# Moving two integer chords of a softmax exponential from VectorE to GpSimd, and sharing TensorE rounds between two groups of heads

## The chip, the cores and the metric

The kernel runs on one core of one Trainium2 chip. The metric is the device time of one execution in microseconds (us), as the median of the runs of a kernel. Each kernel under test was timed next to the kernel before on the same chip. Where runs of different rounds are compared, the kernel before had a median of 788.8 to 789.2 us in each of these rounds. The engines are TensorE (PE in the profile; PEld is its weight load), VectorE (DVE), ScalarE (ACT) and GpSimd (POOL).

## The reference, cut to what matters

One transformer block: layer norm, attention with 32 heads of 16, residual, layer norm, a gated feed-forward layer, residual. 2048 tokens, width 512.

```python
qkv = ...(x @ wqkv)                                # 32 heads of 16
scores = jnp.einsum("bhqd,bhkd->bhqk", q, k) * (Dh ** -0.5)
p = _softmax(scores, axis=-1)                      # 32 x 2048 x 2048 exponentials
o = jnp.einsum("bhqk,bhkd->bhqd", p, v)
...
h = sigmoid(g) * u                                 # F = 1792
```

There are 134 million exponentials. This is what loads ScalarE and VectorE, and the two products around the softmax load TensorE.

## The kernel before

The kernel is a program that plans its own order: while it is built, it keeps a clock per engine (`T["P"]`, `T["D"]`, `T["A"]`, `T["G"]`), adds an assumed duration for each instruction, and from this decides what to issue next. The hardware runs the order that results; it does not see the assumed durations.

A *tile* is (mostly) three *units* of scores in PSUM, each 128 partitions by 512 columns. ScalarE makes the exponentials of two units or of all three in one instruction. Where VectorE has time, it takes the third unit. The kernel computes no exponential there: it writes an affine function of the score as int16 and lets the value product read these bits as fp16, which gives a piecewise linear power of two. Two more copies of it, shifted by +326 and -332 (the *chords*), smooth it: their sum, the last with weight 1.5625, is the exponential. The first exponential and both chords go to TensorE as three inputs, so a unit on VectorE costs TensorE three value products in place of one.

```python
CHORDS, WEIGHT = (326, -332), 1.5625

    GQ, QB = 4, 3                  # four units share a J buffer; three J buffers
    def dexp_first(src, u, n):     # src is PSUM, float32; J is SBUF, int16
        ...
        nc.vector.tensor_scalar(out=J[:, 0, k, :], in0=src, scalar1=ZOFF, scalar2=0.0,
                                op0=ALU.add, op1=ALU.max)
        ...
        if k == GQ - 1:
            dexp_rest()

    def dexp_rest():
        ...
        def chord(s):
            nc.vector.tensor_scalar(out=J[:, s, 0:k, :], in0=J[:, 0, 0:k, :], scalar1=float(CHORDS[s - 1]),
                                    scalar2=0.0, op0=ALU.add, op1=ALU.max)
            for i in range(k):
                quad[i][s].end = T["D"] + TAIL["D"]
        for s in (1, 2):
            chain.append((70 + 133 * k, lambda s=s: chord(s)))
```

A value product has 17 output rows (16 values and the row sum), so four of them, for the four heads of a group, run side by side in four column groups of TensorE (in the timeline their starts lie within 0.02 us of each other). I call such a set a *round*. In the kernel before, a round only takes heads of the current group; at a group's end rounds run with one to three column groups in use.

```python
    def in_rows(uns, limit, full=False):
        ...
            for un in list(left):
                if un.u[3] not in used and len(out) + len(row) < limit:   # u[3]: head 0..3 of the group
                    used.add(un.u[3]); left.remove(un); row.append(un)
            if full and len(row) < live:
                break
```

Four other VectorE instructions are (a) the normalising product of each group, with two SBUF inputs, (b) the two masked copies of each query block, (c) the weighted copy of the value rows, and (d) the application of the second layer norm:

```python
nc.vector.tensor_tensor(out=o2[...], in0=xs[...], in1=rec.to_broadcast(...), op=ALU.mult)              # (a) 60 times
nc.vector.tensor_scalar(out=dst[a][:], in0=qd[:], scalar1=mask[:, a:a + 1], scalar2=None, op0=ALU.mult)  # (b) 30
nc.vector.tensor_scalar(out=Vaug2[:, t], in0=Vaug[:, t], scalar1=WEIGHT, scalar2=None, op0=ALU.mult)     # (c) 16
nc.vector.tensor_scalar(out=hn[:], in0=h[:, i, :], scalar1=mv..., scalar2=rstd..., ...)                  # (d) 14
```

## Time and profile before

| | before |
|---|---|
| median | 788.92 us (788.32 to 789.54, 3 runs) |
| busy share | TensorE 94%, ScalarE 94%, VectorE 90%, GpSimd 4% |
| mean granted TensorE clock | 0.996 |

The page's lines for busy time by engine, and its costliest groups (engine, operation, output and input tile, shapes, count, then busy us and mean ns of one, then idle time just before them):

```profile
PE 740.0 (94%) x11280; PEld 358.3 (45%) x11356; DVE 711.9 (90%) x1406; ACT 737.3 (94%) x780; POOL 31.4 (4%) x67
...
L1321 ACT ACTIVATE pt<-PS 128x1024 f16<-128x1024 f32 (+1 forms) x518 | 541.9, 1138 | 17.8 <-PE PS L1031 11.4
L1177 DVE TENSOR_SCALAR J<-PS 128x512 int16<-128x512 f32 x547 | 363.9, 682 | 34.3 <-PE PS L1154 19.1
...
L1195 DVE TENSOR_SCALAR J<-J 128x2048 int16<-128x2048 int16 (+3 forms) x328 | 185.6, 597 | 1.2
```

The stretch from 200 to 700 us, which is steady attention work (busy us of each engine, number of instructions in brackets; then clock, DMA share, GB/s):

```profile
core 0: us, PE busy (x) PEld busy (x) DVE busy (x) ACT busy (x) POOL busy (x), PEclk, DMA share, GB/s
200.00:700.00 500.00, 479.56 (x8013) 242.64 (x8056) 463.37 (x908) 487.06 (x505) 13.15 (x24) 1.00 0.18 53
```

In 500 us ScalarE works 487, TensorE 480 and VectorE 463. There is no single bound: the plan has filled three engines. The waits view (who waited for whom: us in all, times, longest) shows how little is lost between them:

```profile
ACT pt L1321 <- PE PS L1031: 11.4, 32, 0.7
...
PE PS L1154 <- DVE J L1195: 1.0, 4, 0.3
```

TensorE waited 1.0 us in the whole run for a chord.

### The profile page before, as it was taken

What the parts mean: (1) busy time and instruction counts of PE and PEld (TensorE: products, weight loads), DVE (VectorE), ACT (ScalarE), POOL (GpSimd) and SP (SyncE); (2) the same over time, 40 slices, a digit from 0 to 9 for tenths busy, and PEclk for the clock granted to TensorE, in tenths of its full rate; (3) what the DMA queues carried; (4) which work ended last, traced back from release to release, by engine and by line L of the source; (5) the groups of instructions that cost most, each with busy time, mean ns of one, the idle gap of its engine ahead of it and who ended that gap; (6) DMA issues with size and microseconds to landing.
All of it is one profiled execution on the core that took longest, in us unless ns stands there. A gap on an engine that the chain in (4) does not pass through costs nothing. (4 is left out here: it accounts for less than half of the span.)

```text
span 787.9 us, 25764 instructions
## 1 busy us (share of the span) xinstructions
PE 740.0 (94%) x11280; PEld 358.3 (45%) x11356; DVE 711.9 (90%) x1406; ACT 737.3 (94%) x780; POOL 31.4 (4%) x67
## 2 busy tenths in 40 slices
PE   8889998888999999999999999999999999999997
PEld 3322224444554455444544454435544555444554
DVE  7987999999999899999989899888999898999963
ACT  5989999999999999999999999999999999999962
POOL 4300000001000100000000000100000000100000
PEclk9999999999999999999999999999999999999999
DMA  7000023000131013200312031101211133012160
GB/s 227 1 1 1 1 63 100 3 2 2 56 95 56 9 37 96 61 29 10 95 50 61 16 96 56 37 27 49 83 56 35 36 95 96 8 34 57 56 201 17
DMA packets 66806, 41.56 MB, mean 53 GB/s; under 512 B 3456, under 2 KB 66688, under 8 KB 66688
## 3 DMA queue, kind: packets, MB, share of 16 engines
q1 hardware_dynamic: 66400, 39.59, 16.9%
q8 instruction: 90, 1.47, 0.8%
q10 hardware_dynamic: 288, 0.26, 0.1%
q14 instruction: 28, 0.23, 0.1%
HBM read 37.75 MB, written 2.10 MB: 51 GB/s over the span
## 5 line engine op out<-in xcount | busy, mean ns | idle before, releaser
L1321 ACT ACTIVATE pt<-PS 128x1024 f16<-128x1024 f32 (+1 forms) x518 | 541.9, 1138 | 17.8 <-PE PS L1031 11.4
L1177 DVE TENSOR_SCALAR J<-PS 128x512 int16<-128x512 f32 x547 | 363.9, 682 | 34.3 <-PE PS L1154 19.1
L1154 PE MATMUL PS<-J,Vaug 128*17 128x256 f16 (+1 forms) x2092 | 201.5, 280 | 5.6 <-DVE xs L1097 2.8
L1154 PE MATMUL PS<-pt,Vaug 128*17 128x256 f16 (+1 forms) x2158 | 190.8, 279 | 5.2 <-DVE xs L1097 4.0
L1195 DVE TENSOR_SCALAR J<-J 128x2048 int16<-128x2048 int16 (+3 forms) x328 | 185.6, 597 | 1.2
L1154 PEld LDWEIGHTS <-Vaug 128*17 128x17 bf16 x4886 | 132.9, 90 | 78.3 <-issue 70.8
L1154 PE MATMUL PS<-J,Vaug_100 128*17 128x256 f16 (+1 forms) x1046 | 124.0, 280 | 0.7 <-DVE xs L1097 0.2
L770 PE MATMUL PS<-xnT_82,wgu 128*128 128x256 bf16 x784 | 114.3, 275 | 1.6 <-DVE xnT_82 L761 0.5
L770 PEld LDWEIGHTS <-wgu 128*128 128x128 bf16 x784 | 64.1, 98 | 41.5 <-issue 35.7
L1154 PEld LDWEIGHTS <-Vaug_100 128*17 128x17 bf16 x1046 | 53.6, 90 | 29.6 <-issue 27.3
L1321 ACT ACTIVATE xnT_83<-PS 128x1024 f16<-128x1024 f32 (+1 forms) x52 | 57.4, 1107 | 0.5 <-PE PS L1031 0.4
L788 PE MATMUL PS<-wd,hT 128*128 128x512 bf16 x168 | 50.1, 383 | 2.6 <-issue 2.5
L1031 PEld LDWEIGHTS <-KT_86 32*128 32x128 bf16 x768 | 21.6, 92 | 59.7 <-issue 58.1
L1031 PEld LDWEIGHTS <-KT_87 32*128 32x128 bf16 x1024 | 24.9, 92 | 50.3 <-issue 48.8
L1321 ACT ACTIVATE QTb<-PS 128x1024 f16<-128x1024 f32 x42 | 45.0, 1072 | 0.9 <-PE PS L1031 0.5
L1031 PEld LDWEIGHTS <-KT_88 32*128 32x128 bf16 x1024 | 23.3, 92 | 49.4 <-issue 48.9
L800 ACT ACTIVATE th<-PS 128x512 f32<-128x512 f32 (+1 forms) x63 | 36.4, 577 | 7.5 <-DVE hT L783 6.7
L1031 PE MATMUL PS<-QT_92,KT_87 32*128 32x256 bf16 x512 | 38.2, 272 | 4.5 <-ACT pt L1321 1.9
L1031 PEld LDWEIGHTS <-KT_89 32*128 32x128 bf16 x1024 | 22.8, 92 | 39.4 <-issue 38.9
L1031 PE MATMUL PS<-QT_95,KT_88 32*128 32x256 bf16 x512 | 38.1, 272 | 2.5 <-ACT pt L1321 1.5
L1031 PE MATMUL PS<-QT_93,KT_87 32*128 32x256 bf16 x512 | 37.0, 272 | 2.3 <-ACT pt L1321 1.8
L1031 PE MATMUL PS<-QT_94,KT_88 32*128 32x256 bf16 x512 | 36.1, 272 | 3.0 <-ACT pt L1321 2.5
(288 smaller groups left out, 801.0 us busy)
## 6 DMA issues: line engine op xcount, KB each, us to landing
wgu<-in_B_w_gate_dram SPq DMA_DIRECT2D x49, 256.0 KB, 3.0
wgu<-in_B_w_up_dram SPq DMA_DIRECT2D x49, 256.0 KB, 3.5
out_dram<-ob SPq DMA_DIRECT2D x16, 128.0 KB, 1.7
wd<-in_B_w_down_dram SPq DMA_DIRECT2D x1, 1792.0 KB, 9.2
xr<-in_A_x_dram SPq DMA_DIRECT2D x14, 128.0 KB, 3.5
J<-in_B_w_gate_dram SPq DMA_DIRECT2D x2, 768.0 KB, 4.8
J<-in_B_w_up_dram SPq DMA_DIRECT2D x2, 768.0 KB, 8.2
xb_111<-in_A_x_dram SPq DMA_DIRECT2D x2, 256.0 KB, 4.8
```

The source lines that it names most:

```text
L770: nc.tensor.matmul(ps[:, 0:PARTS[r][2]], lhsT=w[:, d, :], rhs=hn_of(r)[:, d, :], start=(d == 0), stop=(d == DC - 1))
L788: nc.tensor.matmul(ps, lhsT=hT[:, f, i * P:(i + 1) * P], rhs=wd[:, f, :], start=(f == 0), stop=(f == FC - 1))
L800: nc.scalar.activation(out=th[:, 0:ps.shape[-1]], in_=ps, func=ACT.Tanh, scale=0.5)
L1031: nc.tensor.matmul(pss[:, ui, i * CW[qc]:(i + 1) * CW[qc]], lhsT=KT[g // 2][32 * j:32 * j + 32, k * P:(k + 1) * P], rhs=q[32 * j:32 * j + ...
L1154: nc.tensor.matmul(dst[32 * j:32 * j + VW, 0:w], lhsT=un.v[:, kt * SPAN[qc] + i, h, :], rhs=un.ap[:, i * w:(i + 1) * w], start=(c + i == 0 ...
L1177: nc.vector.tensor_scalar(out=J[:, 0, k, :], in0=src, scalar1=ZOFF, scalar2=0.0, op0=ALU.add, op1=ALU.max)
L1195: nc.vector.tensor_scalar(out=J[:, s, 0:k, :], in0=J[:, 0, 0:k, :], scalar1=float(CHORDS[s - 1]), scalar2=0.0, op0=ALU.add, op1=ALU.max)
L1321: ex = nc.scalar.activation(out=pt, in_=pss[:, 0:wa, :], func=ACT.Exp, scale=AS)
```

## The change

The intent: the 328 chord instructions take 185.6 us of VectorE, and GpSimd is 96% idle. If GpSimd makes the chords, VectorE can take more first exponentials (the int16 write from PSUM above) from ScalarE. As the chords then come later, TensorE may fill the rounds of one group's end with heads of the next group, which also saves rounds.

```diff
-    def in_rows(uns, limit, full=False):
+    def in_rows(uns, more, limit, full=False):          # more: units of the next group that are ready
...
+            for un in list(more):
+                j = un.u[3]
+                if (j not in used and len(out) + len(row) < limit
+                        and (due[j] == 0 or not clears and count[gr + (j,)] > 0)):
+                    used.add(j)
+                    more.remove(un)
+                    row.append(un)
...
-                                 rhs=un.ap[:, i * w:(i + 1) * w], start=(c + i == 0),
+                                 rhs=un.ap[:, i * w:(i + 1) * w], start=clears and c + i == 0,
...
+    POOLED, POOL_NS = (1, 2), 470
...
         def chord(s):
+            if s in POOLED:
+                nc.gpsimd.tensor_scalar(out=J[:, s, 0:k, :], in0=J[:, 0, 0:k, :], scalar1=float(CHORDS[s - 1]),
+                                        scalar2=0.0, op0=ALU.add, op1=ALU.max)
+                T["G"] = max(T["G"], quad[-1][0].end + LAT) + POOL_NS * k + 150
+                for i in range(k):
+                    quad[i][s].end = T["G"] + TAIL["G"]
+                return
```

The plan assumes 470 ns for each unit of 512 elements on GpSimd, or 2.03 us for a full chord of four units.

More of the change, by code (lines that the diff above doesn't have):

```diff
@@ L1113, in av_ready, with ahead_ready @@
                 and un.end + LAT <= T["P"] + loose]
-    def in_rows(uns, limit, full=False):
-        out, rows, left = [], 0, list(uns)
-        live = sum(todo[gseq[st["cur"]] + (j,)] > 0 for j in range(4))
-        while left and len(out) < limit:
+    def ahead_ready():
+        i = st["cur"]
+        if i + 1 >= len(gseq) or gseq[i][0] >= NCH:
+            return []
+        j = st["acc"][acc_of(*gseq[i + 1])[1][0]]
+        if j is not None and (j.end is None or j.end + LAT > T["P"] + 60.0):
+            return []
+        return [un for un in avq if un.u[:2] == gseq[i + 1] and un.end is not None
+                and un.end + LAT <= T["P"] + 60.0]
+    def in_rows(uns, more, limit, full=False):
+        out, rows, left = [], 0, list(uns)
+        gr = gseq[st["cur"]]
+        due = {j: todo[gr + (j,)] for j in range(4)}
+        live = 4 if more else sum(n > 0 for n in due.values())
+        more = list(more)
+        clears = more and gseq.index(more[0].u[:2]) % 2 == 0
+        while (left or more) and len(out) < limit:
             row, used = [], set()
@@ L1126, in in_rows @@
                     row.append(un)
-            if full and len(row) < live:
+                    due[un.u[3]] -= 1
+            for un in list(more):
[5 more added lines that the diff above has]
+                    row.append(un)
+            if not row or full and len(row) < live or row[0].u[:2] != gr and len(row) < 4:
                 break
@@ L1133, in av @@
     def av(limit, loose=60.0, full=False):
-        dst, halves = acc_of(*gseq[st["cur"]])
-        busy = [st["acc"][k] for k in halves if st["acc"][k] is not None]
+        busy = [st["acc"][k] for k in acc_of(*gseq[st["cur"]])[1] if st["acc"][k] is not None]
         if any(j.end is None or j.end + LAT > T["P"] + loose for j in busy):
             return 0
-        uns, rows = in_rows(av_ready(loose), limit, full)
+        uns, rows = in_rows(av_ready(loose), ahead_ready(), limit, full)
         if not uns:
@@ L1141, in av @@
         T["P"] = max([T["P"]] + [un.end + LAT for un in uns + busy])
-        for k in halves:
-            st["acc"][k] = None
         for un in uns:
             qc, g, kt, j = un.u
+            dst, halves = acc_of(qc, g)
+            for k in halves:
+                st["acc"][k] = None
             force(("v", kt * SPAN[qc]))
@@ L1152, in av @@
             w = CW[qc]
+            clears = 0 in halves
             for i in range(SPAN[qc]):
                 nc.tensor.matmul(dst[32 * j:32 * j + VW, 0:w], lhsT=un.v[:, kt * SPAN[qc] + i, h, :],
-                                 rhs=un.ap[:, i * w:(i + 1) * w], start=(c + i == 0),
-                                 stop=(todo[qc, g, j] == 0 and i == SPAN[qc] - 1), tile_position=(0, 32 * j))
+                                 rhs=un.ap[:, i * w:(i + 1) * w], start=clears and c + i == 0,
+                                 stop=(todo[qc, g, j] == 0 and i == SPAN[qc] - 1), tile_position=(0, 32 * j),
+                                 skip_group_check=True)
         pe_time("av", MM * rows + 4 * len(uns), 128 * len(uns))
@@ L1160, in av @@
                 un.slot.end = T["P"] + DRAIN
-        qc, g = uns[0].u[:2]
-        if all(todo[qc, g, j] == 0 for j in range(4)):
-            finish_group(qc, g)
+        while st["cur"] < len(gseq) and av_last() == 0:
+            finish_group(*gseq[st["cur"]])
             st["cur"] += 1
@@ L1199, in dexp_rest @@
         for s in (1, 2):
-            chain.append((70 + 133 * k, lambda s=s: chord(s)))
+            if s in POOLED:
+                chord(s)
+            else:
+                chain.append((70 + 133 * k, lambda s=s: chord(s)))
     def pop_chain():
```

## The prediction

> **What bounds it now.** The page gives busy shares of PE 94%, ACT 94%, DVE 90%. By stage (stretch table), from 200 to 700 us ACT is busy 487 of 500 us and PE 479, DVE 463; the granted clock is 0.99 to 1.00. So the attention loop has two saturated engines, TensorE and ScalarE, with VectorE just below; the waits view shows only small waits for VectorE there (PE for the accumulator's transposition 7.5 us in all, PE for the chords J<-J 1.0 us). The last 28 us (tail block) are a serial matmul, tanh and product chain that the change doesn't touch.
>
> **What the change does**, counted in the built instruction orders:
> - VectorE loses 328 chord instructions (185.6 us; 128x2048 takes 0.69 us) and gains 26 first exponentials of 0.68 us (547 to 573; 17.7 us): 712 to about 544 us of work.
> - GpSimd gets the 328 chords (246 of 2048 elements, 32 of 1024, 50 of 512 after regrouping). No chord ran there before. Its one-element TENSOR_SCALAR took 0.34 us. [...]
> - ScalarE: 26 tiles go from 1536 columns (1.50 us) to 1024 (1.06 us): 11.4 us less.
> - TensorE: 94 value matmuls more (each VectorE unit needs three where ScalarE's needs one), but packed better: rounds of up to four column groups fall from 1683 to 1555. A round's starts lie 0.107 us apart in the timeline: 13.7 us less, about 2 us given back to 17 more mode switches.
>
> **How much is on the critical path.** Only the last two: about 11 us on each of the two saturated engines, so about 778 us if idle times stay. The 168 us freed on VectorE are mostly off the path; fewer first exponentials delayed by chord pairs may give some 3 to 5 us of ACT and PE idle back.
>
> Against it: [...] The 60 normalising products (TENSOR_TENSOR, 0.29 us), 32 query splits (0.35 us), 14 layer-norm applies and 16 value copies may each wait about 1 us: perhaps 80 to 100 us on VectorE, most of it absorbed by its new slack, some 5 to 15 us reaching ACT and PE. Chords also arrive 3 to 4 us later than before; the three J buffers are then held longer, and the last group's end may slip 2 us.
>
> Predicted 780 us, 766 to 806. Faster 0.27, same 0.55, slower 0.18.
>
> **What would show it.** GpSimd's J<-J at 2.0 to 2.2 us a full chord, 580 to 630 us busy; VectorE's normalising product and query splits longer than 0.29 and 0.35 us (about 1 us) and bimodal; ACT busy 726 us; PE waits for J from GpSimd under 10 us; first exponentials unchanged at 0.68 us.
>
> **What would make it wrong.** A GpSimd chord of 3 us or more: PE would wait for J and VectorE for free J buffers, 830 us or more. Locked VectorE operations not absorbed: above 800. No blocking and much idle recovered: below 770.

The marked cuts take out of the record the rate on which the forecast of a chord rested, with a second, higher one, and the reason given why VectorE and GpSimd would hold each other up: no trace or run of this case showed them. The sum came to 2.1 us a full chord and some 600 us of GpSimd in all, and the time to 780 us: about 778, with 5 to 15 us of waits and perhaps 2 us at the end against it and 3 to 5 us of idle time for it. The 2 us for 17 mode switches fit the trace: around 400.6 us of the kernel before, the first score product starts 0.21 us after the last round, where rounds start 0.11 us apart. By *blocking* I mean below that a VectorE instruction lasts longer while GpSimd works; a query copy went from 0.35 to 7.16 us in the changed kernel.

## The result, and the profile after

| | before | after |
|---|---|---|
| median | 789.08 us (788.32 to 789.54, 4 runs) | 2160.05 us (2159.68 to 2160.40, 4 runs) |
| ratio | | 2.738 (95% interval 2.733 to 2.742) |
| GpSimd busy | 4% | 95% |
| mean granted TensorE clock | 0.996 | 0.627 |

The changed kernel is 2.74 times as slow, far outside the predicted range of 766 to 806 us.

The page after: busy line, the granted clock in 40 slices, the chain that ended last by engine, and the groups that answer to those shown of before:

```profile
PE 1162.4 (54%) x11373; PEld 427.9 (20%) x11451; DVE 845.3 (39%) x1104; ACT 773.2 (36%) x780; POOL 2057.7 (95%) x411
...
PEclk9865655555565666667566676566556667665557
...
POOL 74%; issue 16%; DVE 5%; PE 4%; ACT 0%; POOLq 0%; DVEq 0%; ACTq 0%
...
L1222 POOL TENSOR_SCALAR J<-J 128x2048 int16<-128x2048 int16 (+3 forms) x344 | 2030.9, 5940 | 43.0 <-DVE J L1203 42.9
L1357 ACT ACTIVATE pt<-PS 128x1024 f16<-128x1024 f32 (+1 forms) x518 | 555.3, 1086 | 1069.1 <-PE PS L1031 1037.4
L1203 DVE TENSOR_SCALAR J<-PS 128x512 int16<-128x512 f32 x573 | 389.1, 686 | 942.8 <-PE PS L1031 587.2
L1179 PE MATMUL PS<-J,Vaug 128*17 128x256 f16 (+1 forms) x2186 | 334.1, 383 | 409.0 <-POOL J L1222 408.2
```

Three things are to be seen. GpSimd is busy 2058 of 2158 us, and 74% of the chain that ended last runs over its chords. Every other engine idles: ScalarE's exponentials now wait for 1069 us in all, the first exponentials on VectorE for 943 us. And the granted TensorE clock, 0.9 or more throughout before, is 0.5 to 0.7 in most slices.

The chords by shape, and who waited:

```profile
L1222 POOL TENSOR_SCALAR J<-J 128x2048 int16<-128x2048 int16 x246 | 1737.6, 7093 | 43.0 <-DVE J L1203 42.9
L1222 POOL TENSOR_SCALAR J<-J 128x1024 int16<-128x1024 int16 x32 | 115.6, 3630 | 0.0
L1222 POOL TENSOR_SCALAR J<-J 128x512 int16<-128x512 int16 x50 | 95.3, 1927 | 0.0
L1222 POOL TENSOR_SCALAR J<-J 128x1536 int16<-128x1536 int16 x16 | 85.8, 5382 | 0.0
```

```profile
ACT pt L1357 <- PE PS L1031: 1037.4, 345, 23.2
PE PS L1179 <- POOL J L1222: 880.0, 276, 10.1
DVE J L1203 <- PE PS L1031: 587.2, 261, 16.9
```

A full chord takes 7.09 us and not 2.0 to 2.2. The four shapes lie on a line: (7093 - 1927) / 1536 = 3.36 ns an element, and about 0.2 us fixed. TensorE waits 880 us for GpSimd where it had waited 1.0 us for VectorE's chords. The kernel issues TensorE's instructions in one order, so the score products (L1031) behind a waiting value product come late too: the other two lines show ScalarE's exponentials and VectorE's first exponentials waiting for them.

The sum closes. 344 chord records at 5.94 us are 2.04 ms, of 2.158 ms. The forecast had the same shapes, but for the 16 of 1536 elements, at 580 to 630 us.

### The profile page after: what moved, and what is told of

The parts are those of the page before. It is cut to its first block, busy times and chain, and to the rows that moved or that the text cites. A ratio compares the mean times of both kernels' runs of the same rounds, so it can differ in the third digit from the quotient of the medians.

```text
span 2157.8 us, 26193 instructions
## 1 busy us (share of the span) xinstructions
PE 1162.4 (54%) x11373; PEld 427.9 (20%) x11451; DVE 845.3 (39%) x1104; ACT 773.2 (36%) x780; POOL 2057.7 (95%) x411
## 4 chain that ended last, share of the span: by engine, by line
POOL 74%; issue 16%; DVE 5%; PE 4%; ACT 0%; POOLq 0%; DVEq 0%; ACTq 0%
POOL J L1222 74%; PE PS L1179 1%; DVE Vaug_100 L297 1%; DVE J L1203 1%; PE PS L770 1%; PE PS L1031 1%; DVE QT_93 L300 1%; DVE Vaug L296 0%; DVE st L260 0%; PE PS L788 0%; PE PS L1504 0%; PE PS L439 0%; DVE QT_95 L300 0%; POOL rstd L268 0%; PE PS L287 0%
## 5 line engine op out<-in xcount | busy, mean ns | idle before, releaser
L1222 POOL TENSOR_SCALAR J<-J 128x2048 int16<-128x2048 int16 (+3 forms) x344 | 2030.9, 5940 | 43.0 <-DVE J L1203 42.9
L1179 PE MATMUL PS<-J,Vaug 128*17 128x256 f16 (+1 forms) x2186 | 334.1, 383 | 409.0 <-POOL J L1222 408.2
L1179 PE MATMUL PS<-J,Vaug_100 128*17 128x256 f16 (+1 forms) x1093 | 192.1, 384 | 472.1 <-POOL J L1222 471.8
L1179 PE MATMUL PS<-pt,Vaug 128*17 128x256 f16 (+1 forms) x2119 | 323.0, 383 | 9.7 <-DVE xs L1097 8.5
L1179 PEld LDWEIGHTS <-Vaug 128*17 128x17 bf16 x4933 | 173.3, 108 | 600.7 <-issue 572.9
L770 PE MATMUL PS<-xnT_82,wgu 128*128 128x256 bf16 x784 | 180.1, 384 | 0.0
L1357 ACT ACTIVATE xnT_83<-PS 128x1024 f16<-128x1024 f32 (+1 forms) x50 | 53.4, 1067 | 77.2 <-PE PS L1031 77.1
L1357 ACT ACTIVATE xnT_84<-PS 128x1024 f16<-128x1024 f32 (+1 forms) x38 | 40.2, 1058 | 70.3 <-PE PS L1031 70.2
L1031 PE MATMUL PS<-QT_92,KT_87 32*128 32x256 bf16 x512 | 55.7, 383 | 17.1 <-DVE J L1203 15.9
L1031 PE MATMUL PS<-QT_94,KT_88 32*128 32x256 bf16 x512 | 52.6, 376 | 12.7 <-DVE J L1203 12.2
L1031 PE MATMUL PS<-QT_97,KT_89 32*128 32x256 bf16 x512 | 51.8, 372 | 11.6 <-DVE J L1203 10.1
L1031 PE MATMUL PS<-QT_96,KT_89 32*128 32x256 bf16 x512 | 51.7, 369 | 9.2 <-DVE J L1203 8.8
L1031 PE MATMUL PS<-QT_95,KT_88 32*128 32x256 bf16 x512 | 52.4, 369 | 6.5 <-DVE J L1203 4.1
L1068 DVE TENSOR_TENSOR o_1_105<-xs,rsum 128x128 bf16<-128x128 f32 x32 | 53.8, 1680 | 1.1
L753 DVE TENSOR_SCALAR hn<-h,mv,rstd 128x512 bf16<-128x512 f32 x14 | 39.2, 2802 | 37.6 <-POOL rstd L268 37.6
```

The source lines that it names most:

```text
L770: nc.tensor.matmul(ps[:, 0:PARTS[r][2]], lhsT=w[:, d, :], rhs=hn_of(r)[:, d, :], start=(d == 0), stop=(d == DC - 1))
L1031: nc.tensor.matmul(pss[:, ui, i * CW[qc]:(i + 1) * CW[qc]], lhsT=KT[g // 2][32 * j:32 * j + 32, k * P:(k + 1) * P], rhs=q[32 * j:32 * j + ...
L1068: nc.vector.tensor_tensor(out=o2[:, 0:w // 32, DH * a:DH * a + DH], in0=xs[:, 0:w // 32, 0:DH], in1=rec.to_broadcast([P, w // 32, DH]), op ...
L1179: nc.tensor.matmul(dst[32 * j:32 * j + VW, 0:w], lhsT=un.v[:, kt * SPAN[qc] + i, h, :], rhs=un.ap[:, i * w:(i + 1) * w], start=clears and ...
L1222: nc.gpsimd.tensor_scalar(out=J[:, s, 0:k, :], in0=J[:, 0, 0:k, :], scalar1=float(CHORDS[s - 1]), scalar2=0.0, op0=ALU.add, op1=ALU.max)
L1357: ex = nc.scalar.activation(out=pt, in_=pss[:, 0:wa, :], func=ACT.Exp, scale=AS)
```

## The experiments

Two theories were on the table at first. Theory A: GpSimd's own time for this instruction is 3.4 times the forecast 2.1 us, and this alone makes the result. Rival B: GpSimd is slow because busy VectorE holds it up. Two more had to be excluded: that the shared rounds do harm, and that the order, planned with a false duration, does the harm. Later the question was what the other terms of the prediction were worth. All kernels gave results that passed the comparison with the reference, but see e5 for how much that says.

### e1: the shared rounds alone

```diff
-    POOLED, POOL_NS = (1, 2), 470
+    POOLED, POOL_NS = (), 470
```

> Changed kernel with both chords back on VectorE: only the sharing of rounds is left. Built order: 1553 rounds of up to four column groups against 1683 (13.9 us of TensorE at 0.107 us a round), 545 first exponentials on VectorE against 547 (ScalarE +0.9 us). If TensorE ends the wait in the loop: about 776 to 780 us. If ScalarE is the nearer bound: 786 to 789 us. If the sharing itself had a hidden cost[...], part of the 2160 us would show here: above 795 us. Theory (GpSimd alone is the cause) says 776 to 789.

Measured: 779.53 us (4 runs) against 788.77; ratio 0.989 (0.987 to 0.990). The page's busy line and the same stretch as above:

```profile
PE 741.4 (95%) x11350; PEld 348.8 (45%) x11350; DVE 708.4 (91%) x1402; ACT 734.9 (95%) x780; POOL 29.7 (4%) x67
```

```profile
200.00:700.00 500.00, 485.31 (x8200) 239.83 (x8197) 471.39 (x921) 493.15 (x514) 12.42 (x24) 1.00 0.19 54
```

The shared rounds are harmless and give 9 us; as an estimate, 130 saved rounds at 0.107 us, the distance of their starts in the timeline, are worth 13.9 us on TensorE. In the stretch, ScalarE went from 487 to 493 us of 500 and TensorE from 480 to 485: the saved rounds let the other engines be used better, until ScalarE has hardly any idle time left. So the whole slowdown comes with the chords on GpSimd.

### e2: one chord on GpSimd

```diff
-    POOLED, POOL_NS = (1, 2), 470
+    POOLED, POOL_NS = (2,), 470
```

> Only the third chord on GpSimd (118 full chords and smaller ones, 578 units of 512). Theory A, GpSimd's own rate of 0.164 us + 3.36 ns an element bounds the kernel: 1.02 ms of GpSimd work, span 1100 us if VectorE's second chords don't get in the way; if each of them ([...]0.69 us alone) waits[...] until a GpSimd chord ends, they show some 4 to 7 us each and the span is 1150 to 1350 us. Rival B, GpSimd is slow because of the traffic of the other engines: the full chord is clearly not 7.05 us here, as VectorE is busier than in the changed kernel.

Measured: 1435.45 us, one run. That is above the expected 1150 to 1350. The groups by shape:

```profile
L1222 POOL TENSOR_SCALAR J<-J 128x2048 int16<-128x2048 int16 x118 | 860.9, 7301 | 256.5 <-DVE J L1203 225.3 <-DVE rsum L1067 31.3
...
L1228 DVE TENSOR_SCALAR J<-J 128x2048 int16<-128x2048 int16 x118 | 317.7, 2694 | 1.7
```

The GpSimd chord is 7.30 us here against 7.09, though VectorE is busy for 79% of the span and not 39% (holds included): nothing for rival B. The new fact is the second line. VectorE's own full chord took 0.69 us before and takes 2.69 us on average here (up to 7.58 us), in a run in which GpSimd is busy for 76% of the span and not 4%: it is held. I had expected 4 to 7 us for each; the median over all shapes is only 0.93 us, so at least half were hardly held. The span is longer than expected: GpSimd sat idle 256 us before its full chords, 225 of them waiting for a first exponential on VectorE. That the two take turns fits this, but no run separates it.

### e3: a plan with the true duration

```diff
-    POOLED, POOL_NS = (1, 2), 470
+    POOLED, POOL_NS = (1, 2), 1720
```

> Both chords on GpSimd, but the kernel's planner is told 1720 ns a unit in place of 470. It then gives VectorE 361 first exponentials in place of 573 and ScalarE the rest (about +80 us against before). Theory A: GpSimd work 722 units x 1.72 us = 1.27 ms, span 1290 to 1360 us, GpSimd above 93% busy, chord still 7.05 us. If the 2160 us came from a bad order (the plan's wrong figure) more than from the rate: span near ScalarE's 820 us.

Measured: 1443.76 us, one run; GpSimd busy 1307.8 us (91%), full chord 7.09 us. With the true figure the plan gives VectorE 361 units in place of 573, and the time falls by a third, because a good third less is asked of GpSimd (722 units in place of 1146). It stays far from ScalarE's 824 us. So the plan's wrong figure is not the cause: the order can only choose how many chords to pay for. The time is above the expected 1290 to 1360 us and GpSimd's share below the expected 93%: the estimate left out 134 us in which GpSimd did nothing, 75 of them waiting for VectorE's first exponentials.

### e4: single GpSimd instructions, behind the end of the kernel

Behind the end of the kernel before, a row of instructions on scratch tiles:

```diff
+    ts(I16, I16, 2048)                          # add, max: the chord
+    ts(I16, I16, 1024)
+    ts(I16, I16, 2048, op1=None)                # add alone
+    ts(I16, I16, 2048, op1=None, op0=ALU.max)   # max alone
+    G.tensor_copy(out=dst[I16][:], in_=src[I16][:])
+    ts(BF16, BF16, 2048); ts(FP16, FP16, 2048); ts(FP32, FP32, 2048); ts(I32, I32, 2048) ...
+    G.tensor_tensor(out=dst[I32][:, 0:1024], in0=src[I32][:, 0:1024], in1=src[I32][:, 1024:2048], op=ALU.add) ...
```

> The kernel before, with a row of single GpSimd instructions behind its end, where every other engine is idle. Theory A: int16 add+max of 2048 elements again 7.0 to 7.1 us, of 1024 elements 3.6 us; it is the engine's own cost. Rival B (contention with a busy VectorE): about 2.1 us here. What makes it slow is then read from the neighbours: if it is the int16 type, fp32 of 2048 is near 2 us; if it is two operations in one, one operation takes half; if it is the general rate of the instruction, all take 7 us. Last four pairs: a VectorE instruction that may start only when a 7 us GpSimd chord has begun. [...]

Measured, in the timeline view (start us, duration us; three of the first five lines of the diff: the chord, the addition alone, the copy):

```profile
784.80 7.12 POOL L1500 TENSOR_SCALAR dst<-src 128x2048 int16<-128x2048 int16 x1 [96.88 <-DVE src L1496]
```

```profile
795.72 5.37 POOL L1500 TENSOR_SCALAR dst<-src 128x2048 int16<-128x2048 int16 x1
```

```profile
806.60 1.89 POOL L1506 COPY dst<-src 128x2048 int16<-128x2048 int16 x1
```

And in the groups by shape, the other types and the two-input additions:

```profile
L1500 POOL TENSOR_SCALAR dst<-src 128x2048 f16<-128x2048 f16 x1 | 7.1, 7084 | 0.0
...
L1500 POOL TENSOR_SCALAR dst<-src 128x1024 f32<-128x1024 f32 x1 | 3.6, 3632 | 0.1
L1500 POOL TENSOR_SCALAR dst<-src 128x1024 int16<-128x1024 int16 x1 | 3.6, 3626 | 0.1
L1518 POOL TENSOR_TENSOR dst<-src 128x2048 f32<-128x2048 f32 x1 | 3.6, 3600 | 0.0
...
L1517 POOL TENSOR_TENSOR dst<-src 128x1024 int32<-128x1024 int32 x1 | 2.3, 2337 | 0.0
```

Theory A holds and rival B falls. During the first chord (7.12 us) VectorE was still filling scratch tiles, but the fp16 instruction (7.08 us) had all other engines idle. The type does not matter: with two operations int16 takes 7.12 and fp16 7.08 us, and bf16, fp32 and int32 have a mean of 6.22 to 6.23 us over one instruction with two operations and one with one, as 7.08 and 5.37 us give. The number of operations does: 5.37 us with one, 7.1 us with two, and a plain copy of the same elements takes 1.89 us. A quarter of this last figure is 0.47 us for 512 elements, the value that the plan assumed for a chord.

The last part of this run, meant to show VectorE waiting, failed: its instructions became ready 0.04 us *before* the chord started, not after, and so went first. It shows only the reverse: behind the bf16 tensor_scalar and behind the product of two SBUF inputs the chord lasts a little longer (7.19 and 7.32 us), behind the product with an input in PSUM and behind the reduction it does not (7.08 us both). What VectorE suffers is read from the other runs.

### e5: the same order, with GpSimd as fast as predicted

```diff
-                nc.gpsimd.tensor_scalar(out=J[:, s, 0:k, :], in0=J[:, 0, 0:k, :], scalar1=float(CHORDS[s - 1]),
-                                        scalar2=0.0, op0=ALU.add, op1=ALU.max)
+                nc.gpsimd.tensor_copy(out=J[:, s, 0:k, :], in_=J[:, 0, 0:k, :])
```

> The changed kernel with each GpSimd chord replaced by a plain copy of the same elements (the probe: 1.89 us for 2048 against 7.08 us). Wrong result on purpose: the chord's offset is missing. The order of all engines is the changed kernel's, instruction for instruction. It asks whether the rest of the prediction holds once the one wrong term, the chord's duration, is what the prediction took (about 2.1 us). If yes: 770 to 790 us, GpSimd about 560 us busy, VectorE's normalising product and query splits lengthened to about 1 us (at most some 100 us together), PE's waits for GpSimd under 30 us. If blocking[...] costs more than the prediction allowed: above 800 us.

Measured: 806.93 us (4 runs); ratio to before 1.022 (1.020 to 1.024). The result lacks the offsets on purpose, yet it passed the comparison, so "correct" is a weak statement for the softmax's fine shape in this case.

This run answers the most useful question: with the one wrong term put right, was the rest of the prediction right? Only partly. GpSimd was busy 571.8 us, near the predicted 580 to 630 (a full copy took 1.91 us and not 2.1), TensorE waited only 2.2 us for its results, and the time came down from 2160 to 807 us. But it is 27 us above e1, where I had predicted 780 and a loss of 5 to 15 us to blocking. One place of many, in the timeline view, copied in part:

```profile
525.85 0.19 DVE L1067 RECIPROCAL rsum<-xs 128x8 f32<-128x8 f32 x1
...
525.98 0.28 PE L1179 MATMUL PS<-pt,Vaug 128*17 128x256 f16 x1
526.07 5.75 POOL L1222 COPY J<-J 128x2048 int16<-128x2048 int16 x4 [2.37 <-DVE rsum L1067]
...
526.08 2.02 DVE L1068 TENSOR_TENSOR o<-xs,rsum 128x128 bf16<-128x128 f32 x1
...
528.03 0.68 DVE L1203 TENSOR_SCALAR J<-PS 128x512 int16<-128x512 f32 x1
...
528.76 0.37 PE L1031 MATMUL PS<-QT,KT 32*128 32x256 bf16 x2 [1.15 <-DVE J L1203]
...
531.41 1.02 ACT L1356 ACTIVATE pt<-PS 128x1024 f16<-128x1024 f32 x1 [2.29 <-PE PS L1031]
...
531.70 0.42 PE L1179 MATMUL PS<-xnT,Vaug 128*17 128x256 f16 x1
```

GpSimd's copy starts at 526.07. VectorE's normalising product, 0.29 us alone, starts 0.01 us later and lasts 2.02 us. The first exponential behind it starts at 528.03; the score product that needs its PSUM space waits 1.15 us, and ScalarE then idles for 2.29 us. After the gap TensorE's matmuls take 0.42 us and not 0.28, and rounds start 0.21 us apart and not 0.11; the granted clock from 530 to 534 us is 0.67 (columns as in the stretch of before):

```profile
530.00:534.00 4.00, 4.00 (x47) 1.35 (x46) 1.61 (x3) 1.88 (x2) 1.82 (x2) 0.67 0.00 0
```

The products of the whole run, in e1 and then in this run:

```profile
L1068 DVE TENSOR_TENSOR o<-xs,rsum 128x128 bf16<-128x128 f32 x56 | 16.4, 292 | 1.9
```

```profile
L1068 DVE TENSOR_TENSOR o<-xs,rsum 128x128 bf16<-128x128 f32 x56 | 51.5, 920 | 1.9
```

Over the run the four kinds of VectorE instruction named above lose about 65 us (product 18 to 56, query copies 10 to 31, applies 8 to 12, value rows 5 to 8 us in sum). That is less than the 80 to 100 us predicted. But the run stands 27 us above e1, where 5 to 15 us were predicted for this. Whether the blocking makes these 27 us, e8 to e12 ask.

### e6 and e7: a right result at the faster rate

The probe shows a cheaper chord: an int32 addition of two packed int16 values at a time. The maximum can go if the first exponential is floored at 332 in place of 0 (as an fp16 number, 2e-5).

```diff
-                nc.gpsimd.tensor_scalar(...add, max...)
+                nc.gpsimd.tensor_tensor(out=J[:, s, 0:k, :].bitcast(I32), in0=J[:, 0, 0:k, :].bitcast(I32),
+                                        in1=step2[...].to_broadcast([P, k, QC // 2]), op=ALU.add)
...
-        nc.vector.tensor_scalar(out=J[:, 0, k, :], in0=src, scalar1=ZOFF, scalar2=0.0,
+        nc.vector.tensor_scalar(out=J[:, 0, k, :], in0=src, scalar1=ZOFF, scalar2=float(-CHORDS[1]),
-    POOLED, POOL_NS = (1, 2), 470
+    POOLED, POOL_NS = (1, 2), 545          # e7: (1,), 545, and no floor
```

> Right result wanted: both chords stay on GpSimd, as int32 additions of two packed values at a time (the probe: 2.34 us for 1024 int32), no maximum, because the first exponential is floored at 332 in place of 0. Planner told 545 ns a unit. Built order: 547 first exponentials, 1523 rounds. GpSimd 316 additions, about 640 us busy. If the rate was the whole trouble: 770 to 780 us, level with or up to 1% below sharing rounds alone (779.5). If blocking and the later chords cost what the freed VectorE gives: 780 to 795 us.

> Only the second chord (plus 326) packed on GpSimd, the third on VectorE as before; GpSimd about 330 us busy. Built order: 576 first exponentials, 1574 rounds, ScalarE about 12 us less work than before. Now VectorE's own chord (0.69 us[...]) can meet a GpSimd addition of 2.3 us: expected mean of the VectorE chord 0.9 to 1.6 us. If that is absorbed: 768 to 778 us, the best so far; if not, 780 to 800 us.

Measured: e6 822.33 us (ratio 1.041, 1.039 to 1.043), e7 821.04 us (ratio 1.041, 1.039 to 1.043), 5 runs each. The packed addition took 1.91 us in e6, where the second input is one element read again and again, and 2.34 us in the probe, with two full inputs. Both kernels are slower than before all the same, and above what I expected. In e7 VectorE's own full chord went from 0.69 to 1.03 us, within the expected range, and GpSimd was busy only 334 us, and still the kernel is 32 us slower than before and 41.5 us slower than e1. No twin of e7 with the products and query copies moved away was run, so its cause is argued from the longer chords alone. In e6 the PSUM wait seen above is the telling one (the first line is VectorE's wait for J buffers that value products still read):

```profile
DVE J L1208 <- PE PS L1179: 71.6, 57, 4.8
...
ACT pt L1363 <- PE PS L1031: 27.6, 47, 2.9
...
PE PS L1031 <- DVE J L1208: 14.4, 21, 2.1
```

### e8, e9 and e10: VectorE kept clear of GpSimd, first attempt

If blocking is the cost, it should go when the VectorE instructions that grew beside GpSimd in e5 (means: products 0.29 to 0.92 us, query copies 0.34 to 1.07, value rows 0.30 to 0.47) are taken away. Three edits: product (a) goes to GpSimd, query copies (b) and value rows (c) are made straight from PSUM, as the first exponentials are, which took 0.68 us in e1 and in e5.

```diff
-            nc.vector.tensor_tensor(out=o2[...], in0=xs[...], in1=rec.to_broadcast(...), op=ALU.mult)
+            nc.gpsimd.tensor_tensor(out=o2[...], in0=xs[...], in1=rec.to_broadcast(...), op=ALU.mult)
-            nc.vector.tensor_scalar(out=dst[a][:], in0=qd[:], scalar1=mask[:, a:a + 1], ...)
+            nc.vector.tensor_scalar(out=dst[a][:], in0=ps, scalar1=maskz[:, a:a + 1], ...)
-        nc.vector.tensor_scalar(out=Vaug2[:, t], in0=Vaug[:, t], scalar1=WEIGHT, ...)
+        nc.vector.tensor_scalar(out=Vaug2[:, t, :, 0:DH], in0=ps..., scalar1=WEIGHT, ...)
+    nc.gpsimd.memset(Vaug2[:, :, :, DH:VW], 0.5 * WEIGHT)
```

> e5_copy (806.9 us) with VectorE's instructions that can meet GpSimd[...] taken out of the loop: the normalising product goes to GpSimd itself, the query splits and the weighted value rows are made straight from PSUM (one SBUF operand at most). Only 14 layer-norm applies are left. Wrong result on purpose, as e5_copy. Theory: the 27 us between e5_copy and e1_rows_only (779.5) come from VectorE instructions held by a GpSimd instruction and what follows from them (late first exponential, PE waiting[...]). Then: 775 to 790 us, no VectorE instruction of the loop above 0.8 us but the applies, granted clock back above 0.993, ScalarE's waits for the scores down from 33 us to under 18. Rival: the order planned with GpSimd (chords arriving later) costs it: 800 to 810 us still.

> The same with the right result: packed int32 additions on GpSimd in place of the copies (1.91 us a full chord in e6_packed, as a copy), planned at 470 ns a unit. Same order of instructions as e8_copy_free, so theory and rival expect the same as there: 775 to 790, or 800 and more. Below 779 it would be the best version of all.

> Control: e1_rows_only with the same three edits, chords on VectorE. It shows what the edits alone cost or give: VectorE loses 60 products (18 us) and gains some 10 us for splits and 6 us for value rows from PSUM. Expected within 8 us of e1_rows_only: 774 to 788 us.

Measured: e8 802.09 us (4 runs), e9 801.26 us (5), e10 800.20 us (4). Taken alone, e8 would have spoken for the rival (800 to 810). The control forbids this reading: without any chord on GpSimd it is at 800 us too, 21 us worse than e1, outside what I expected. Its stretches show where (e10 first, then e1):

```profile
0.00:40.00 40.00, 32.34 (x181) 11.98 (x181) 30.20 (x67) 24.11 (x31) 14.87 (x32) 0.83 0.36 112
40.00:80.00 40.00, 32.38 (x196) 9.94 (x194) 28.11 (x52) 27.92 (x29) 3.11 (x8) 0.87 0.00 1
```

```profile
0.00:40.00 40.00, 34.70 (x240) 13.97 (x241) 35.05 (x88) 30.11 (x37) 15.73 (x39) 1.00 0.36 112
40.00:80.00 40.00, 38.04 (x292) 10.70 (x291) 32.58 (x63) 36.55 (x37) 0.00 (x0) 1.00 0.00 1
```

In the first 80 us ScalarE did 52 us of work, against 67 in e1, and the clock was below 1. Edit (c) had put a second GpSimd memset of 2.6 us before the first layer norms, whose square roots this kernel takes on GpSimd. The trace shows less than I made of it: the first root starts 1.9 us later and ScalarE's first exponential 1.3 us later. The same edit also took the weighted value rows from 0.30 to 0.68 us each and raised the plan's figure for them, and in these 80 us TensorE's waits for value rows grew (its weight loads from 2.5 to 7.7 us, its products from 1.9 to 5.0). Which of these cost most was not separated. The experiment was spoilt by a side effect of its own edit, but the pair e8 and e10 already differs by only 2 us.

### e11 and e12: VectorE kept clear of GpSimd, second attempt

Edit (c) and its memset were taken out again. (A build of the control reused a buffer too early. Telling the plan 450 ns for the product in place of 500 gave an order without it, for both.)

> e9_packed_free without the edit to the value rows (the control e10 lost some 14 us in the first 80 us: two GpSimd memsets there delayed the first layer norms), right result. Only the products (to GpSimd) and the query splits (from PSUM) are kept away[...]. If VectorE instructions held by GpSimd were what separated e6_packed (822) from e1_rows_only (779.5): 770 to 784 us, and within 8 us of its control e12. If the later chords are the cost: 795 us or more.

> Control of e11: shared rounds with the chords on VectorE and the same two edits. The first 80 us are again those of e1_rows_only. 561 first exponentials against 545, 1553 rounds: 770 to 782 us.

Measured: e11 786.20 us (ratio 0.997, 0.995 to 0.998), e12 781.96 us (ratio 0.991, 0.990 to 0.993), 5 runs each. e11 came 2 us above the expected range and e12 on its edge; both are within 8 us of each other as the theory asked. The waits that stood at 71.6 and 14.4 us in e6:

```profile
DVE J L1216 <- PE PS L1187: 79.6, 57, 4.7
...
ACT pt L1371 <- PE PS L1033: 12.9, 26, 2.2
...
PE PS L1033 <- DVE J L1216: 0.9, 3, 0.5
```

| | chords on VectorE | chords on GpSimd | difference |
|---|---|---|---|
| products and query copies on VectorE, from SBUF | e1 779.5 | e5 806.9 (copies), e6 822.3 (packed) | 27.4, 42.8 us |
| products on GpSimd, query copies from PSUM | e12 782.0 | e11 786.2 (packed) | 4.2 us |
| value rows from PSUM too (spoilt first 80 us) | e10 800.2 | e8 802.1 (copies), e9 801.3 (packed) | 1.9, 1.1 us |

So of the 27 to 43 us that fast chords on GpSimd cost, some 23 to 39 us go when products and query copies are moved. The lower figure is the safer one: e5 was planned with 470 ns a unit like e11, e6 with 545. The pair with the spoilt start says the same for the copies (27.4 to 1.9 us). That the chords come later is no rival for this part: VectorE's wait for J buffers is longer in e11 (79.6 us) than in e5 (68.8) and e6 (71.6), while the time is shorter. The comparison is not perfectly clean: each edit makes the plan choose a somewhat different order (547 first exponentials in e6, 573 in e5, 563 in e11), and the 15 us between e5 and e6 were not taken apart. What is shown is that blocking is the larger part. The fastest kernel of all is e1, with no chord on GpSimd.

## Why the prediction was right or wrong

**What bounds the kernel: right.** TensorE and ScalarE together held the loop, and VectorE's freed time was off the path. e1 relieved TensorE alone and gained 9 us; e11, with VectorE busy for 567 us, is no faster than e12 with 707 us. No run relieved ScalarE alone.

**Instruction counts: right, but for 16.** 26 units moved from ScalarE to VectorE, and the 328 chords (with the 16 of 1536 elements, which I left out of the list: 344) went to GpSimd. ScalarE's exponentials of three units fell from 118 to 91, those of two rose from 571 to 599. That its busy time rose from 737 to 773 us is no contradiction: busy time is the time covered, and the instructions overlap less here. The 518 exponentials into pt, taken one by one (count times mean), last 589 us before and cover 542; they last 563 us after and cover 555. In e5 they last 577 us and cover 536, and ScalarE's busy time was 730 us, against 726 predicted.

**"GpSimd's J<-J at 2.0 to 2.2 us a full chord, 580 to 630 us busy": wrong. This is the step that failed.** A full chord took 7.09 us in the changed kernel and 7.12 us behind the end of the kernel (e4), so 2031 us in all, and GpSimd became the bound; VectorE had taken 0.69 us for the same chord. The sum joined the duration of a one-element instruction in the trace, 0.34 us, with a time per element that no trace or run showed. Measured, it is 3.36 ns an element. Only a copy, at 1.89 us, comes near the forecast. The plan's figure of 470 ns a unit, 2.03 us a full chord, is a quarter of the measured time of a copy, not of a chord; nothing in the profile before supported it.

**"What would make it wrong: a GpSimd chord of 3 us or more: PE would wait for J" : right in kind.** TensorE waited 880 us for GpSimd. The consequence was larger than "830 us or more", because GpSimd alone needs 2.06 ms, and TensorE, idle for long stretches, also ran at a granted clock of 0.627 on average.

**Blocking: right in kind, wrong in size.** The instructions that I named grew; the statistics (684 to 683 ns, median) and the first exponentials (682 to 686 ns, mean) did not. Why these and not those was not shown. Minimum, median and maximum in ns, after the number, of the query copies that grew most and of the statistics of the second layer norm, before and after:

```profile
L300 DVE TENSOR_SCALAR QT_97<-qd,mask x4: 349/350/353, 112.5 to 602.0; 128x512 bf16<-128x512 bf16 x4
```

```profile
L300 DVE TENSOR_SCALAR QT_97<-qd,mask x4: 6561/7156/7207, 192.0 to 1658.3; 128x512 bf16<-128x512 bf16 x4
```

```profile
L260 DVE BATCH_NORM_STATS2 st<-h x14: 652/684/694, 191.5 to 685.9; 128x6 f32<-128x512 f32 x14
```

```profile
L260 DVE BATCH_NORM_STATS2 st<-h x14: 650/683/695, 479.3 to 1884.4; 128x6 f32<-128x512 f32 x14
```

A query copy of 0.35 us took 7.16 us, the length of a chord, while the statistics stayed at 0.68 us. Over all 30 query copies the mean went from 0.35 to about 4.0 us, so many were held for part of a chord only. In the changed kernel the four kinds lost about 250 us together, mostly off the path since GpSimd was the bound anyway. At the predicted rate (e5) they lost 65 us, less than the 80 to 100 us predicted, but "some 5 to 15 us reaching ACT and PE" was too small: the run stood 27 us above e1, of which blocking is the larger part. So even with the rate put right the time, 807 us, is just above the predicted range: this is a second, smaller step that failed. The estimate treated a held instruction as lost VectorE time that slack can absorb. In the place shown, the held product stands in front of a first exponential whose PSUM space TensorE needs; TensorE stops 1.5 us and ScalarE 3.0 us after the product started, and the clock of the 4 us from 530 us on is 0.67. How the 27 us divide between such gaps and the lower clock was not measured.

**"About 778 us if idle times stay": reached, but by half of the change.** e1 gives 779.5 us without a chord on GpSimd. It lacks the 11 us on ScalarE that the sum counted on, so the agreement is partly luck and no proof of the sum.

## What to carry to other kernels

Before moving work to an engine that has never done it in this kernel, measure that very instruction, with its number of operations, on otherwise idle engines; a one-element instance (0.34 us here, against 7.09 us for the chord), a rate that no run has shown and a constant in a planner are no measurement. An idle engine is not free when its work holds up the instructions of a full one (a query copy went from 0.35 to 7.16 us here): look in a trace for the full engine's instructions that grow, and ask what stands behind them in its queue. And keep a control for every edit that removes a wait: here an unnoticed side effect of 20 us would have reversed the verdict.
